# Local and global attention followed by a gated FFN: the gate and value products of the first three FFN blocks are taken during the first half chunk's attention

## The chip, the cores and the metric

The kernel runs on one core of one Trainium2 chip. The metric is the device time of one execution in microseconds (us), as the median of several runs. A core has five engines with queues of their own: TensorE (PE in the profile, with PEld for its weight loads), VectorE (DVE), ScalarE (ACT), GpSimd (POOL) and SyncE (SP), which here issues all DMA transfers. Each queue runs in order.

## What is computed

Eight batches with eight heads each: 512 local queries of width 64 attend to a band of 32 positions to either side and to 32 global keys; 32 global queries attend to all 544 keys. The result, 4,352 rows (8 x 544) of width 512, goes through a gated FFN with 1,536 hidden units.

```python
s_ll = np.where(np.abs(pos[:, None] - pos[None, :]) <= 32, scale * q_l @ k_l.T, -1e9)
a_l = sm(np.concatenate([scale * q_l @ k_g.T, s_ll], axis=-1))
out_l = a_l @ np.concatenate([v_g, v_l])
out_g = sm(scale * q_g @ k_all.T) @ v_all
x = concat([out_g, out_l]).transpose(0, 2, 1, 3).reshape(B * S, H * D)
out = (1 / (1 + np.exp(-(x @ w_gate))) * (x @ w_val)) @ w_out
```

The FFN weights arrive as float64 words and are turned into pairs of float32 parts (high and low) on the chip; a product is the sum of three matmuls: high by high, low by high, high by low.

## The kernel before, in words

**Chunks and blocks.** The local rows are cut into chunks: chunk 0 and chunk 1 are the two halves (256 rows each) of batch 0, chunks 2 to 8 are batches 1 to 7 (512 rows each), and a last chunk of 256 rows holds the global rows. The FFN of a chunk has twelve blocks of 128 hidden units (NF = 12). One FFN item is one chunk and one block f: 12 matmuls into `bank_g` and 12 into `bank_v` (L399: three combinations of parts by four slices kt of the width), the gate on ACT and DVE (L407 to L414: tanh, min, exp, abs), the merge (L419 to L423: two multiplications on DVE, a rounding copy on ACT, a subtraction on DVE, giving `hh`), and one item later the output products (L436) into `bank_o`. Chunk 0 runs eight blocks ahead (`lead`), then chunk 1 its first eight, then both take turns.

**Attention.** A head of chunk 0 is one `local_unit` of four steps: scores (L233), the row minimum on DVE and the exponential on ACT (L247, L250); sums and division (L253, L254, L217) into `p_buf`; transposes on PE (L269) and a copy on ACT (L277); the product with the values (L292, L293) and a copy (L296). After each pair of heads `x_split` (L371 on ACT, L372 on POOL) makes the two parts of slice kt of the FFN's input x: pair kt gives slice kt. In chunk 0 a `fill` of one float32 128x128 matmul stands after three of the four steps, and eight fills stand at the start (L110).

**Converting weights.** `convert` turns one 128x1024-word piece into its two parts: a Prelu on ACT (L136), a shift and a shift-and-or on DVE (L138, L139), a rounding copy on ACT (L140) and a subtraction on POOL (L141). There are 36 pieces (gate, value and output of each block), 512 KB each, in a ring of three staging buffers; when a piece is converted, the load of the piece three places later is issued on SP (`stage`, L126). Output pieces are written back to DRAM (L152, L153) and loaded for use as `wo` (L427).

**The order.** Everything but the FFN items is an event with a due time; `ffn_stream` yields after each group of matmuls how much FFN work it was (4.5 for a half chunk's item), and events that are due by then are emitted in between. Chunk 0's attention is due from -1000 on, four units a head, so that all of it comes before the first FFN item at 0; chunk 1's attention is due from 1 to about 21, chunk 2's from 23 on. The pieces of block 0 are due at -985, -980 and -977, those of block f at -2 + 4f and after. This gives the order of emission; the framework then orders each engine's queue at build time by its own estimate of what is ready, with earlier emitted work first, and `issue_after(ins)` holds an instruction behind `ins` on its engine.

**PSUM.** Eight banks: four for a ring `att`, shared by `bank_x`, `bank_y` (attention), `bank_g` and `bank_v`, and `bank_o0` to `bank_o3`, in which output rows of chunk 0 (o0, o1) and chunk 1 (o2, o3) are summed. Until the first output product these four hold nothing but what the fills write (into o3).

Of the kernel before, what the change touches and what calls it, by code (L numbers as in the profile page):

```python
# [8 lines left out]
F32 = mybir.dt.float32  # L9
# [38 lines left out]
CONVERT = (-2, 4, 1, 3)  # L48
CONVERT_EARLY = (-985, -980, -977)
# [10 lines left out]
def kernel(ctx, tc, qk, v, w_gate, w_val, w_out, out_l, out_g):  # L60
# [45 lines left out]
    fill_ps = ps.tile([P, DM], F32, name="bank_o3")  # L106
# [4 lines left out]

    fill(FILL[0])
# [3 lines left out]
    w_src = []  # L116
    for f in range(NF):
        ws = slice(2 * f * P, 2 * (f + 1) * P)
        w_src += [w.rearrange("(t p) f -> p t f", p=P)[:, :, ws] for w in (w_gate, w_val)]
        w_src.append(w_out[f * P:(f + 1) * P, :].rearrange("(t p) m -> p t m", p=P))  # L120
# [7 lines left out]
    def convert(i, hi, lo):  # L128

        src = w_src[i]  # L130
        t, n = src.shape[1], src.shape[2] // 2
        st, v = (o[i % len(o)].rearrange("p (t n) -> p t n", t=t) for o in conv_bufs)
        words = st.rearrange("p t (n two) -> p t n two", two=2)
        low, high = words[:, :, :, 0], words[:, :, :, 1]
        vf, hf = v.bitcast(F32), high.bitcast(F32)
        nc.scalar.activation(hf, hf, AF.Prelu, scale=2.0 ** -112, alpha=-2.0 ** 32)  # L136
        with tc.issue_after(anchor[0].ins) if i < 3 else nullcontext():
            nc.vector.tensor_scalar(v, low, 29, None, op0=ALU.logical_shift_right)  # L138
            nc.vector.scalar_tensor_tensor(v, high, 3, v, op0=ALU.logical_shift_left, op1=ALU.bitwise_or)  # L139
        nc.scalar.copy(hi, vf)  # L140
        nc.gpsimd.tensor_tensor(lo, vf, hi.bitcast(F32), op=ALU.subtract)  # L141
        stage(i + len(conv_bufs[0]))

    def convert_w(f, i):
        fs = slice(f * P, (f + 1) * P)
        w = (wg, wv)[i]
        convert(3 * f + i, w[0][:, :, fs], w[1][:, :, fs])

    def convert_wo(f):
        hi, lo = (spl.tile([P, 1, DM], F32R, name=nm, tag="kl") for nm in ("wo_hi", "wo_lo"))  # L150
        convert(3 * f + 2, hi, lo)
# [61 lines left out]
    def scaled(kind, out, in_, by):  # L213
        if NORM[kind][cnt["norm"] % len(NORM[kind])] == "s":
            nc.scalar.mul(out, in_, by)
        else:
            nc.vector.tensor_scalar(out, in_, by, None, op0=ALU.mult)  # L217
# [164 lines left out]

    def ffn_stream(items):

        prev = None
        later = []
        wo = None
        for n_it in range(len(items) + 1):
            if n_it < len(items):  # L390
# [3 lines left out]
                for w, nm in ((wg, "bank_g"), (wv, "bank_v")):  # L394
# [9 lines left out]
                    if nm == "bank_g":  # L404
                        th = ffn.tile([P, 512], F32, name="th", bufs=1)[:, 0:ntok]
                        mn = ffn.tile([P, 512], F32, name="mn", bufs=1)[:, 0:ntok]
                        nc.scalar.activation(th, acc, AF.Tanh, scale=0.5)  # L407
                        if n_it < 2 * NF and n_it % 2:
                            nc.scalar.activation(mn, acc, AF.Relu, scale=-1.0)
                            nc.scalar.activation(mn, mn, AF.Exp, scale=-1.0)  # L410
                        else:
                            nc.vector.tensor_scalar(mn, acc, 0.0, None, op0=ALU.min)  # L412
                            nc.scalar.activation(mn, mn, AF.Exp)  # L413
                        last_th = nc.scalar.activation(th, th, AF.Abs)  # L414
                        while later:
                            store_out(*later.pop(0), after=last_th)
                    else:

                        nc.vector.tensor_tensor(acc, acc, mn, op=ALU.mult)  # L419
                        nc.vector.scalar_tensor_tensor(acc, th, 1.0, acc, op0=ALU.add, op1=ALU.mult)  # L420
                        hh = ffn.tile([P, 2, 512], F32R, name="hh", bufs=2)
                        nc.scalar.copy(hh[:, 0, 0:ntok], acc)  # L422
                        nc.vector.tensor_tensor(hh[:, 1, 0:ntok], acc, hh[:, 0, 0:ntok].bitcast(F32), op=ALU.subtract)  # L423
                    yield ntok / 512
                if not (wo is not None and items[n_it - 1][1] == f):
                    wo = ffn.tile([P, 2, DM], F32R, name="wo", bufs=2)
                    nc.sync.dma_start(wo.bitcast(F32), wo_dram[f])  # L427
            if prev is not None:
                C2, f2, ph, pwo = prev
                nt = C2["ntok"] // P  # L430
                if f2 == 0:
                    C2["o"] = [ps.tile([P, DM], F32, name=f"bank_o{C2['o0'] + t}") for t in range(nt)]
                o_ps = C2["o"]
                for i, (a, c) in enumerate(((0, 0), (1, 0), (0, 1))):
                    for t in range(nt):
                        nc.tensor.matmul(o_ps[t], ph[:, a, t * P:(t + 1) * P], pwo[:, c],  # L436
                                         start=f2 == 0 and i == 0, stop=f2 == NF - 1 and i == 2)
                    if f2 == NF - 1 and i == 2:
                        for t in range(nt):
                            if t >= 2 and n_it < len(items):  # L440
                                later.append((C2, t))
                            else:
                                store_out(C2, t)
                    yield nt / 4
            prev = (C, f, hh, wo) if n_it < len(items) else None
# [85 lines left out]
    a0, step, *d = CONVERT  # L531
    for f in range(NF):
        at = a0 + f * step
        g, v_, o = CONVERT_EARLY if f == 0 else (at, at + d[0], at + d[1])
        queue.append((g, 4, lambda f=f: convert_w(f, 0)))
        queue.append((v_, 4, lambda f=f: convert_w(f, 1)))
        queue.append((o, 4, lambda f=f: convert_wo(f)))
# [79 lines left out]
```

## Time and profile before

| | |
|---|---|
| median of 3 runs | 1186.67 us (1185.14 to 1191.4) |
| the profiled execution | 1188.97 us, span of its instructions 1187.1 us |
| first matmul of an FFN item | 38.49 us after the span's start |
| busy, share of the span | PE 97%, PEld 81%, DVE 65%, ACT 64%, POOL 35% |
| granted TensorE clock, mean | 0.997 |

Times within the profile count from the span's start. A row of the timeline is: start, duration from the first start to the last end, engine, line, operation, output and inputs with the shape, count; in brackets the idle time of that engine just before, and what ended it. A float32 matmul of the attention is two passes and counts as two. A row of the windows is: stretch, its length, then busy time and count for PE, PEld, DVE, ACT and POOL, the granted clock, the busy share of the DMA engines and what they moved in GB/s.

### The profile page before, as it was taken

The page shows a single profiled execution, that of the slowest core. Times are in us where ns is not written, and L with a number is a line of the kernel's source. Part 1 is how long each engine was busy: PE and PEld are TensorE (multiplying, and loading weights), DVE is VectorE, ACT ScalarE, POOL GpSimd, SP SyncE. Part 2 cuts the span into 40 slices and gives each one's busy share as a digit, 9 for nine tenths or more (in the row PEclk, how much of TensorE's full clock was granted, in tenths as well). Part 3 has the DMA queues.
Part 4 walks back from the last instruction along what each step waited for, and adds up shares of the span by engine and source line. Part 5 has one row for each costly group of instructions (what it writes and reads, how often), then busy time and mean ns, then how long its engine had stood idle before and what let it go on. Part 6 is the DMA issues. An engine that isn't in the chain of part 4 may idle for free.

```text
span 1187.1 us, 19115 instructions
## 1 busy us (share of the span) xinstructions
PE 1150.8 (97%) x6596; PEld 963.8 (81%) x6596; DVE 776.9 (65%) x2132; ACT 755.0 (64%) x1737; POOL 412.4 (35%) x408
## 2 busy tenths in 40 slices
PE   8898999999999999999999999999999999999998
PEld 6666888888888888887788888888788888888897
DVE  5767756666776676667776677677676677633343
ACT  5897777666666666666666666576665675532333
POOL 1434344424442444434443444434353443100000
PEclk9999999999999999999999999999999999999999
DMA  8787853333333333443333443343443342132143
GB/s 292 251 277 260 260 161 115 115 105 111 115 98 128 115 97 106 115 128 98 109 111 110 115 115 97 106 129 97 115 115 105 112 115 72 49 107 71 54 147 120
DMA packets 59489, 151.81 MB, mean 128 GB/s; under 512 B 6144, under 2 KB 19456, under 8 KB 59392
## 3 DMA queue, kind: packets, MB, share of 16 engines
q1 hardware_dynamic: 59392, 150.59, 41.7%
q8 instruction: 52, 0.85, 0.3%
q14 instruction: 45, 0.37, 0.1%
HBM read 135.36 MB, written 15.20 MB: 127 GB/s over the span
## 4 chain that ended last, share of the span: by engine, by line
PE 70%; DVE 10%; ACT 5%; issue 2%; POOL 1%; DMA 0%; ACTq 0%; DVEq 0%; POOLq 0%
PE bank_v L399 19%; PE bank_g L399 19%; PE bank_o L436 19%; DVE p_buf L217 4%; PE bank_y L269 3%; PE bank_x L233 3%; ACT s_sb L250 3%; PE bank_x L300 2%; PE bank_x L301 2%; PE bank_x L317 1%; PE bank_x L360 1%; DVE t L304 1%; DVE mn L412 1%; DVE bank_v L419 1%; DVE bank_v L420 1%
## 5 line engine op out<-in xcount | busy, mean ns | idle before, releaser
L399 PE MATMUL bank_v<-xt,wv 128*128 128x512 f32 (+1 forms) x1440 | 327.8, 364 | 14.7 <-DVE pt L281 14.4
L399 PE MATMUL bank_g<-xt,wg 128*128 128x512 f32 (+1 forms) x1440 | 331.1, 365 | 1.1 <-DVE hh L423 0.8
L436 PE MATMUL bank_o<-wo,hh 128*128 128x512 f32 x1224 | 330.2, 401 | 0.9 <-ACT hh L422 0.9
L399 PEld LDWEIGHTS bank_v<-xt,wv 128*128 128x128 f32 x1440 | 237.0, 189 | 51.8 <-issue 16.4
L399 PEld LDWEIGHTS bank_g<-xt,wg 128*128 128x128 f32 x1440 | 237.3, 189 | 38.7 <-issue 2.7
L436 PEld LDWEIGHTS bank_o<-wo,hh 128*128 128x128 f32 x1224 | 217.7, 189 | 40.9 <-ACT hh L422 1.8
L250 ACT ACTIVATE s_sb<-s_sb,nm 128x192 f32<-128x192 f32 (+1 forms) x240 | 110.4, 461 | 98.5 <-DVE nm L247 97.6
L217 DVE TENSOR_SCALAR p_buf<-s_sb,r 128x128 f32<-128x128 f32 (+2 forms) x443 | 152.4, 381 | 6.3 <-PE bank_y L269 1.7
L305 POOL TENSOR_TENSOR x<-t 64x256 f32<-64x256 f32 x104 | 76.4, 735 | 173.1 <-DVE t L304 147.0
L210 POOL TENSOR_TENSOR vhl<-v_raw,vhl 128x512 fp32r<-128x512 f32 x52 | 67.2, 1293 | 186.6 <-ACT vhl L209 98.9
L197 POOL TENSOR_TENSOR kl<-qk_raw,qk_hi 128x704 fp32r<-128x704 f32 x52 | 88.6, 1704 | 109.7 <-ACT qk_hi L196 109.2
L422 ACT CAST hh<-bank_v 128x512 fp32r<-128x512 f32 (+1 forms) x120 | 62.7, 523 | 95.4 <-DVE bank_v L420 94.6
L407 ACT ACTIVATE th<-bank_g 128x512 f32<-128x512 f32 (+1 forms) x120 | 63.8, 532 | 85.9 <-PE bank_g L399 85.5
L412 DVE TENSOR_SCALAR mn<-bank_g 128x512 f32<-128x512 f32 (+1 forms) x108 | 67.4, 624 | 72.5 <-ACT th L407 72.5
L304 DVE TENSOR_TENSOR t<-bank_x,t 64x512 f32<-64x512 f32 x104 | 70.7, 680 | 61.9 <-ACT t L303 61.2
L419 DVE TENSOR_TENSOR bank_v<-bank_v,mn 128x512 f32<-128x512 f32 (+1 forms) x120 | 73.6, 613 | 56.6 <-PE bank_v L399 49.8
L247 DVE CUSTOM_DVE_ANT_0 s_sb<-bank_x,masks 128x192 f32<-128x192 f32 (+1 forms) x240 | 79.8, 369 | 37.6 <-PE bank_x L233 32.5
L423 DVE TENSOR_TENSOR hh<-bank_v,hh 128x512 fp32r<-128x512 f32 (+1 forms) x120 | 72.9, 608 | 36.5 <-ACT hh L422 34.6
L199 POOL TENSOR_TENSOR qk_hi<-qk_raw,qk_hi 64x256 fp32r<-64x256 f32 x104 | 80.1, 790 | 4.1
L269 PE MATMUL bank_y<-ident,p_buf 128*128 128x128 f32 x440 | 70.3, 274 | 5.5 <-DVE p_buf L217 3.6
L420 DVE SCALAR_TENSOR_TENSOR bank_v<-th,bank_v 128x512 f32<-128x512 f32 (+1 forms) x120 | 73.2, 610 | 1.8
L413 ACT ACTIVATE mn<-mn 128x512 f32<-128x512 f32 (+1 forms) x108 | 62.9, 582 | 15.8 <-DVE mn L412 11.1
(108 smaller groups left out, 1656.1 us busy)
## 6 DMA issues: line engine op xcount, KB each, us to landing
wo<-wo_dram SPq DMA_DIRECT2D x116, 512.0 KB, 3.4
qk_raw<-in_qk_dram SPq DMA_DIRECT2D x104, 312.0 KB, 4.4
v_raw<-in_v_dram SPq DMA_DIRECT2D x52, 256.0 KB, 2.7
out_dram<-ob SPq DMA_DIRECT2D x34, 256.0 KB, 3.1
xt<-in_w_gate_dram SPq DMA_DIRECT2D x12, 512.0 KB, 5.3
xt<-in_w_val_dram SPq DMA_DIRECT2D x12, 512.0 KB, 5.2
xt<-in_w_out_dram SPq DMA_DIRECT2D x12, 512.0 KB, 4.8
v_nat<-in_v_dram SPq DMA_DIRECT2D x8, 512.0 KB, 7.1
```

Of the source, the lines that this page charges most:

```text
L197: nc.gpsimd.tensor_tensor(kl, t[:, K0:Q1], hi[:, K0:Q1].bitcast(F32), op=ALU.subtract)
L199: nc.gpsimd.tensor_tensor(hi[64:128, r], t[64:128, r], hi[64:128, r].bitcast(F32), op=ALU.subtract)
L217: nc.vector.tensor_scalar(out, in_, by, None, op0=ALU.mult)
L247: anchor[0] = nc.vector.tensor_tensor_reduce(out=s_sb[:, i, w], in0=s_ps[:, i, w], in1=mid[:, w], scale=-0.125, scalar=3.0e38, op0=ALU.add ...
L250: exp_at[0] = nc.scalar.activation(s_sb[:, i, w], s_sb[:, i, w], AF.Exp, bias=nm[:, i:i + 1], scale=-1.0, accum_out=sm[:, i:i + 1])
L269: nc.tensor.transpose(pt_ps[:, t], flat[:, t * P:(t + 1) * P], ident)
L304: nc.vector.tensor_tensor(t0, o_ps[0:64], t0, op=ALU.add)
L399: nc.tensor.matmul(acc, w[a][:, t, fs], xt[:, c, t, x0:x0 + ntok], start=n == 0, stop=n == 11)
L412: nc.vector.tensor_scalar(mn, acc, 0.0, None, op0=ALU.min)
L419: nc.vector.tensor_tensor(acc, acc, mn, op=ALU.mult)
L420: nc.vector.scalar_tensor_tensor(acc, th, 1.0, acc, op0=ALU.add, op1=ALU.mult)
L436: nc.tensor.matmul(o_ps[t], ph[:, a, t * P:(t + 1) * P], pwo[:, c], start=f2 == 0 and i == 0, stop=f2 == NF - 1 and i == 2)
```

## The change

The gate and value products of blocks 0, 1 and 2 for chunk 0 leave the FFN stream. They are taken slice by slice as soon as a pair of heads has given its slice of x (`pre_products`, 6 matmuls for block and slice, 72 in all), and are summed in banks o2, o3 and o1, gate and value side by side in one bank. Since the sums of a bank are then spread over time, each of the three banks is first set to zero by a float32 matmul of `ident` with the zeroed `p_bufs[0]` (128x512). The fills go to o0.

The FFN stream starts with the gates and merges of the three blocks, then takes block 3; the output products of blocks 0 and 1 stand between block 3's gate and value products, that of block 2 after them. Chunk 0's output banks o0 and o1 are opened by block 0's output products, and o1 held block 2's sums. Items 3 to 20 yield 0.5 more each (9 in all, what the 72 matmuls yielded), so that from item 21 on the due times meet the same items as before.

The six gate and value pieces of the three blocks are converted and loaded first, due from -992.9 to -975.5; the output pieces of blocks 0 and 1 follow at -971.5 and -967.5, that of block 2 at -2, block 3 from -3 on and each later block four units after the one ahead. For the first three pieces the Prelu is now held behind the exponential that was emitted last (before it was free), and the DVE steps are held behind the last division step or row minimum (before, the last row minimum). `gate_parts`, `merge`, `load_wo` and `out` hold the code that stood in the stream, with the same instructions.

```diff
-CONVERT = (-2, 4, 1, 3)
-CONVERT_EARLY = (-985, -980, -977)
+CONVERT = (-3, 4, 1, 3)
+PRE = 3
+PRE_AT = (-992.9, -991.5, -987.5, -983.5, -979.5, -975.5)
+PRE_OUT = (-971.5, -967.5, -2)
...
-    fill_ps = ps.tile([P, DM], F32, name="bank_o3")
+    fill_ps = ps.tile([P, DM], F32, name="bank_o0")
...
+    pre_banks = []
+    for i in (2, 3, 1)[:PRE]:
+        bank = ps.tile([P, 2, 256], F32, name=f"bank_o{i}")
+        nc.tensor.matmul(bank, ident, p_bufs[0], start=True, stop=False)
+        pre_banks.append(bank)
     fill(FILL[0])
...
-        nc.scalar.activation(hf, hf, AF.Prelu, scale=2.0 ** -112, alpha=-2.0 ** 32)
+        with tc.issue_after(exp_at[0].ins) if i < 3 else nullcontext():
+            nc.scalar.activation(hf, hf, AF.Prelu, scale=2.0 ** -112, alpha=-2.0 ** 32)
...
-            nc.vector.tensor_scalar(out, in_, by, None, op0=ALU.mult)
+            anchor[0] = nc.vector.tensor_scalar(out, in_, by, None, op0=ALU.mult)
...
+    def pre_products(f, kt):
+        C = chs[0]
+        ntok, x0, xt = C["ntok"], C["x0"], C["xt"]()
+        fs = slice(f * P, (f + 1) * P)
+        bank = pre_banks[f]
+        for i, w in enumerate((wg, wv)):
+            for n, (a, c) in enumerate(((0, 0), (1, 0), (0, 1))):
+                nc.tensor.matmul(bank[:, i], w[a][:, kt, fs], xt[:, c, kt, x0:x0 + ntok],
+                                 start=False, stop=kt == KT - 1 and i == 1 and n == 2)
...
+        for f in range(PRE):
+            half = slice(256 * (f % 2), 256 * (f % 2) + 256)
+            bank = pre_banks[f]
+            hh = hhs[f // 2][:, :, half]
+            gate_parts(bank[:, 0], th[:, half], mn[:, half], f % 2)
+            merge(bank[:, 1], th[:, half], mn[:, half], hh)
+            pend.append((chs[0], f, hh, lambda f=f: wos[f]))
-        for n_it in range(len(items) + 1):
+        for n_it in range(PRE, len(items) + 1):
...
+                        if n_it == PRE:
+                            yield from out(False)
+                            wos[2] = load_wo(2)
+                            yield from out(False)
...
+            if n_it < 7 * PRE:
+                yield 0.5
...
+    for f in range(PRE):
+        for kt in range(KT):
+            at = max(-1000 + START["per0"] * (2 * kt + 1) + STAGES[-1] + 0.5, PRE_AT[2 * f + 1])
+            queue.append((at, 5, lambda f=f, kt=kt: pre_products(f, kt)))
```

More of the change, by code (lines that the diff above doesn't have):

```diff
@@ L383, in ffn_stream, with load_wo, out @@
+    def load_wo(f):
+        t = ffn.tile([P, 2, DM], F32R, name="wo", bufs=2)
+        nc.sync.dma_start(t.bitcast(F32), wo_dram[f])
+        return t
     def ffn_stream(items):
-        prev = None
+        pend = []
         later = []
         wo = None
-        for n_it in range(len(items) + 1):
+        def out(last):
+            C, f, hh, wo = pend.pop(0)
+            nt = C["ntok"] // P
+            if f == 0:
+                C["o"] = [ps.tile([P, DM], F32, name=f"bank_o{C['o0'] + t}") for t in range(nt)]
+            for i, (a, c) in enumerate(((0, 0), (1, 0), (0, 1))):
+                for t in range(nt):
+                    nc.tensor.matmul(C["o"][t], hh[:, a, t * P:(t + 1) * P], (wo() if callable(wo) else wo)[:, c],
+                                     start=f == 0 and i == 0, stop=f == NF - 1 and i == 2)
+                if f == NF - 1 and i == 2:
+                    for t in range(nt):
+                        if t >= 2 and not last:
+                            later.append((C, t))
+                        else:
+                            store_out(C, t)
+                yield nt / 4
+        th = ffn.tile([P, 512], F32, name="th", bufs=1)
+        mn = ffn.tile([P, 512], F32, name="mn", bufs=1)
+        hhs = [ffn.tile([P, 2, 512], F32R, name="hh", bufs=2) for _ in range(2)]
+        wos = {f: load_wo(f) for f in range(2)}
+        for f in range(PRE):
[6 more added lines that the diff above has]
+        for n_it in range(PRE, len(items) + 1):
@@ L424, in ffn_stream @@
                     yield ntok / 512
                 if not (wo is not None and items[n_it - 1][1] == f):
[L426 to L444, printed above, removed]
@@ L445, in ffn_stream @@
-            prev = (C, f, hh, wo) if n_it < len(items) else None
+                    wo = load_wo(f)
+            if pend:
+                yield from out(n_it >= len(items))
+            if n_it < len(items):
+                pend.append((C, f, hh, wo))
+            if n_it < 7 * PRE:
+                yield 0.5
     def att_events(ci, start, per, tail=0):
@@ L530 @@
         queue.append((9 * NF * (ci - 2) + (START["x2"] if ci == 2 else 0), -1, new_x))
[L531 to L537, printed above, removed]
+    for t_, f, kind in order:
+        queue.append((t_, 4, (lambda f=f, k=kind: convert_w(f, k)) if kind < 2 else (lambda f=f: convert_wo(f))))
+    for f in range(PRE):
+        for kt in range(KT):
+            at = max(-1000 + START["per0"] * (2 * kt + 1) + STAGES[-1] + 0.5, PRE_AT[2 * f + 1])
+            queue.append((at, 5, lambda f=f, kt=kt: pre_products(f, kt)))
     queue.append((-1002, 2, lambda: [stage(i) for i in range(3)]))
```

51 lines of the change are left out of this document (32 added, 19 removed).

## Prediction

> **What bounds the kernel now.** I read the page first, then the busy times by stage, then PE's timeline from the start to the second FFN item, then ACT, DVE and POOL beside it. The change touches nothing behind the items of the two half chunks, so these carry the argument.
>
> ```profile
> span 1187.1 us, 19115 instructions
> PE 1150.8 (97%) x6596; PEld 963.8 (81%) x6596; DVE 776.9 (65%) x2132; ACT 755.0 (64%) x1737; POOL 412.4 (35%) x408
> ```
>
> ```profile
> 0.00:38.50 38.50, 31.19 (x193) 24.55 (x193) 25.44 (x96) 23.49 (x63) 10.20 (x19) 1.00 0.81 276
> 38.50:60.00 21.50, 20.70 (x127) 15.85 (x127) 14.00 (x42) 19.45 (x55) 8.85 (x8) 1.00 0.84 265
> ...
> 110.00:115.00 5.00, 3.12 (x18) 1.93 (x17) 4.99 (x12) 3.52 (x13) 2.80 (x2) 0.93 0.88 307
> 115.00:120.00 5.00, 5.00 (x17) 3.25 (x15) 2.60 (x9) 2.53 (x9) 1.27 (x1) 0.50 0.14 23
> 120.00:125.00 5.00, 5.00 (x33) 4.51 (x32) 2.03 (x6) 4.14 (x12) 0.31 (x1) 0.88 0.96 318
> ```
>
> The columns behind the length are PE, PEld, DVE, ACT, POOL, then clock, DMA share and GB/s. The first 38.5 us, chunk 0's attention, I call the prelude. PE is busy 31.19 us of it and idle 7.31. In the stage behind it PE is busy for 20.70 of 21.50 us and ACT for 19.45: both are nearly full, so PE work taken out of that stage shortens it, as long as ACT follows. What matters is whether the prelude has room for that work.
>
> ```profile
> 3.81 1.76 PE L233 MATMUL bank_x<-qk_nat 64*128 64x192 f32 x8 [3.81 <-DMA qk_nat<-in_qk_dram]
> 5.50 4.60 PE L110 MATMUL bank_o<-ident 128*128 128x128 f32 x26
> 11.04 0.49 PE L269 MATMUL bank_y<-ident,p_buf 128*128 128x128 f32 x2 [0.95 <-DVE p_buf L217]
> ...
> 18.12 0.97 PE L233 MATMUL bank_x<-qk_nat 64*128 64x192 f32 x4
> 19.02 0.49 PE L110 MATMUL bank_o<-ident 128*128 128x128 f32 x2
> ...
> 21.54 0.97 PE L233 MATMUL bank_x<-qk_nat 64*128 64x192 f32 x4
> ...
> 32.38 0.74 PE L269 MATMUL bank_y<-ident,p_buf 128*128 128x128 f32 x3 [0.78 <-DVE p_buf L217]
> 32.97 1.06 PE L110 MATMUL bank_o<-ident 128*128 128x128 f32 x8
> 35.12 0.43 PE L292 MATMUL bank_x<-pt_nat,v_nat 128*64 128x128 f32 x2 [1.10 <-ACT pt_nat L277]
> ...
> 37.47 0.43 PE L292 MATMUL bank_x<-pt_first,v_nat 128*64 128x128 f32 x2 [0.68 <-ACT pt_first L277]
> 38.49 0.62 PE L399 MATMUL bank_g<-xt,wg 128*128 128x256 f32 x3
> 39.04 0.97 PE L233 MATMUL bank_x<-qk_nat 64*128 64x224 f32 x4
> 40.14 1.48 PE L399 MATMUL bank_g<-xt,wg 128*128 128x256 f32 x9
> 41.46 1.11 PE L399 MATMUL bank_v<-xt,wv 128*128 128x256 f32 x8
> 42.51 1.05 PE L317 MATMUL bank_x<-qk_nat 64*32 64x256 f32 x4
> ...
> 43.54 0.74 PE L399 MATMUL bank_v<-xt,wv 128*128 128x256 f32 x4
> ```
>
> From one head's scores (18.12) to the next (21.54) a head takes 3.42 us of PE, and no row of the timeline between them shows a wait; three fills of two passes, such as the one at 19.02, are among its work. After the empty start (3.81 us) the bracketed waits are 0.95, 0.78, 1.10 and 0.68 us. So I take PE to be the bound of the prelude too. Work moved there is then carried, not hidden, but for these waits.
>
> **The change, part by part.** *The products in the prelude.* 72 matmuls of 128x256, in twelve groups of six. Where twelve of them run back to back later, one costs 0.12 us:
>
> ```profile
> 228.41 1.44 PE bank_g L399 x12
> ```
>
> So 8.64 us is the least if PE is full. The dearest row is the first triple, 0.55 us from 38.49 to 39.04, 0.18 us each, 13.2 us in all. A group of six is nearer to the run of twelve; its six matmuls are 0.72 us by that row and 1.1 by the triples, and I take 0.82, an estimate near the run with some 0.1 us for the change of shape: **+9.8 us**.
>
> *The zeroing.* Three float32 matmuls of 512 columns and two passes, 3,072 columns, now stand ahead of the eight fills. The 26 early passes (3,328 columns) are thirteen fills, eight of the start and five drawn forward from the heads. Zeroing and eight fills are 5,120 columns: 4.60 us for the first 3,328 as now, and 1,792 at the price of the row of 32.97 (1,024 columns in 1.06 us), 1.85 us, so they end at 11.95 instead of 10.10. Transposes began at 11.04: 0.9 us later, and of the five fills, which come later now (ten passes, 1.3 us), I put half on the path. **+1.5 us**; nothing if the zeroing runs in the empty time before 3.81, 4.2 us if all its columns come at the early price.
>
> *The first Prelu behind the exponentials.* ACT stands still for the first weights before it takes the first exponential, though the first scores were done by 5.57 us (3.81 + 1.76):
>
> ```profile
> 8.69 0.68 ACT L136 ACTIVATE xt<-xt 128x512 f32<-128x512 f32 x1 [6.67 <-DMA xt<-in_w_gate_dram]
> 9.27 0.44 ACT L250 ACTIVATE s_first<-s_first,nm 128x192 f32<-128x192 f32 x1
> ```
>
> Held behind, the Prelu lets the exponentials begin up to 3 us sooner. PE gains only its 0.95 us wait by that, for zeroing and fills are next in its queue until 11.95; that wait is in the sum above. Nothing further: **0**.
>
> *The waits filled.* 0.78, 1.10 and 0.68 us, with products at hand to fill them: **-2.6 us** (bounds 0 and -2.6). Prelude: 9.8 + 1.5 - 2.6 = +8.7; block 3 starts at 47.2 instead of block 0 at 38.49.
>
> *The stage behind.* Block 0's 24 matmuls take 0.55 (to 39.04), 2.37 (40.14 to 42.51) and 0.74 us, 3.66 together. Three blocks: **-11.0 us**; -8.6 at the price of the run of twelve.
>
> *The gates in a bunch.* Three gates and merges now start together, and block 0's output product waits for all three, since bank o1 held block 2.
>
> ```profile
> 42.74 0.36 ACT L407 ACTIVATE th<-bank_g 128x256 f32<-128x256 f32 x1
> ...
> 43.74 0.41 ACT L414 ACTIVATE th<-th 128x256 f32<-128x256 f32 x1
> 44.06 0.40 ACT L413 ACTIVATE mn<-mn 128x256 f32<-128x256 f32 x1
> ```
>
> 0.36 + 0.41 + 0.40, and 0.36 for the merge's copy, of the same size as the tanh: 1.53 us of ACT a block, 4.6 for three. Over it lie block 3's 24 matmuls (2.9 us) and chunk 1's first head (0.97 and 1.05 us): 4.9. With the latency between engines I take **+0.5 us**, 0 to 2; without the cover it would be 4.6.
>
> *The weight pieces.* The same pieces, transfers and stores. SP's order changes only in which piece is behind which, and value and gate pieces of blocks 1 and 2 pass the output pieces of 0 and 1. A wait of a load on the ring holds back what is behind it on SP, attention inputs of chunk 1, which have the whole longer prelude to land. ACT has 15 us free in the prelude (38.50 - 23.49) and can take some pieces earlier; in return later pieces are due one block or more sooner. **0**, with 2 us either way.
>
> Sum: 8.7 - 11.0 + 0.5 = **-1.8 us**. The profiled execution took 1188.97 us, 1.9 around its span and 2.3 above the median of the runs; on the median that is **1184.9 us**, 0.15% less. A measurement of this kernel can tell about 0.5% (5.9 us) from no change, so this is the same.
>
> **Rivals.** *A, the prelude has room.* PE's busy time counts pipelined matmuls from start to end and can hide gaps between small passes. By weight loads PE is busy only 24.55 of 38.50 us, 13.95 free, 10.1 without the empty start, more than the 9.8 of the products. If all of it can be used, the sum is 1.5 - 11.0 + 0.5 = -9.0: 1177.7 us. For it: most passes there are short. Against it: the regular 3.42 us with no wait. The Trainium skill, Perfetto Trace Analysis, section Identifying the Most-Contended Engine, calls matmul busy time a poor measure of headroom and weight-load busy time a better one; by that rule this rival would be the forecast.
>
> *B, the half clock is gone.* From 110 to 125 us the granted clock falls to 0.93, 0.50 and 0.88: 0.35 + 2.5 + 0.6 = 3.45 us lost, right behind a stretch with PE busy 3.12 of 5. All that is shifted now; if no such gap comes up, -1.8 - 3.5 = -5.3: 1181.4 us, about at the edge of what can be told.
>
> *C, slower: PE stands at the products for the low parts from POOL.* A group needs the low part of x and of the weights, and in PE's queue the attention of later heads stands behind it.
>
> ```profile
> 18.77 0.41 ACT L371 CAST xt<-x 128x256 fp32r<-128x256 f32 x1
> 19.26 0.73 POOL L372 TENSOR_TENSOR xt<-x,xt 128x256 fp32r<-128x256 f32 x1 [16.90 <-ACT xt L371]
> 29.78 1.27 POOL L141 TENSOR_TENSOR wo_lo<-xt,wo_hi 128x512 fp32r<-128x512 f32 x1 [1.26 <-ACT pt_first L277]
> 29.84 2.91 DVE L217 TENSOR_SCALAR p_buf<-s_first,r 128x128 f32<-128x128 f32 x4
> ```
>
> After a pair of heads a group can wait 0.41 for ACT, 1.27 for a weight piece ahead on POOL, 0.73 for its own: 2.4 us, 9.6 for four pairs: -1.8 + 9.6 = +7.8, 1194.5 us. It is slower from (5.9 + 1.8) / 4 = 1.9 us a pair on, that is if hardly any work of the next heads stands ahead of the groups. Against it: the build-time order puts ready work ahead, and the first pieces come earlier than now. In its favour, POOL also slows DVE: the four divisions at 29.84 take 2.91 us beside POOL's pieces, and more pieces now fall into the prelude. The Trainium skill, SBUF — State Buffer, section Who interferes with whom, has the shared port of the two as an exclusive lock for a whole instruction; the trace agrees (2.91 us for four), and by it every further piece can cost DVE its 1.27 us.
>
> *D, it doesn't do what it says.* The products, ready or not, are all put behind the last pair. Then the 2.6 us of waits stay: +0.8, 1187.5 us. The due times are spread over the pairs, which speaks against it.
>
> **How the numbers follow.** Forecast 0.36 (its own range 1181.5 to 1189, from the bounds of zeroing, waits and bunch), A 0.32, B 0.08, C 0.17, D 0.07. Faster by over 0.5%: A and half of B, 0.36. Slower: C, 0.17. Within: the rest, 0.47. The range leaves out the far end of A and of C: 1176 to 1193 us.
>
> **What would show it.** Right: block 3's first gate matmul at about 47 us; hardly a bracketed wait of over 0.5 us on PE between 12 and 47; a head step of 3.4 us plus 0.8 for each group in it; ACT's first exponential near 6.5 us; the steady chunks behind unchanged. A: block 3 before 43 us. C: waits of groups on xt, wg or wv from POOL, or a clock under 1.00 before 50 us. The forecast is wrong if the stage behind doesn't give back the 11 us because ACT, already at 90% there, holds block 3 and the following gates.

## The result, and the profile after

The changed kernel takes 1196.93 us (median of five runs, 1194.67 to 1197.88), the kernel before 1186.67 us (1184.95 to 1191.4). The ratio is 1.007 (95% interval 1.0049 to 1.0092): the change makes the kernel slower by 0.7%, where no change (1184.9 us, in a range of 1176 to 1193) was forecast.

The page of the changed kernel, for the lines that opened the prediction:

```profile
span 1192.8 us, 19122 instructions
PE 1157.6 (97%) x6602; PEld 968.5 (81%) x6602; DVE 778.5 (65%) x2132; ACT 755.2 (63%) x1737; POOL 413.8 (35%) x408
```

The span is 5.7 us longer, and PE is busy 6.8 us longer. PE's six instructions more are the zeroing passes. The first matmul of chunk 2's first item, which I call the mark, comes at 244.81 us after the change and at 238.01 before, 6.8 us later; behind it the two kernels do the same work, and the change makes up 1.1 us. The windows up to the mark, of the changed kernel first, with its prelude:

```profile
0.00:47.11 47.11, 41.69 (x252) 31.86 (x253) 33.03 (x105) 29.48 (x73) 16.45 (x24) 1.00 0.82 274
0.00:244.81 244.81, 227.79 (x1513) 185.33 (x1513) 160.62 (x481) 179.41 (x485) 93.18 (x91) 0.97 0.66 210
```

```profile
0.00:238.01 238.01, 220.53 (x1506) 180.76 (x1507) 158.67 (x481) 179.30 (x485) 92.38 (x91) 0.99 0.67 216
```

PE's idle time, length less busy time, is 17.02 us after and 17.48 before. So the change did not make PE wait longer in all; it made PE busy 7.26 us longer, with a lower granted clock (0.97 for 0.99). Some 3.4 us of this are the clock: in the trace of the changed kernel it stands at half four times for 3.4 us, 6.8 us lost, in that of the kernel before once for 6.8 us, 3.4 us lost. The rest is of the size of the zeroing (5.03 us, the row of L117 below). The reader should take from this that a summed idle time says nothing of what the waits do to the clock behind them.

**The start.** PE, DVE and ACT of the changed kernel:

```profile
5.54 5.03 PE L117 MATMUL bank_o<-p_buf,ident 128*128 128x512 f32 x6
10.40 2.39 PE L112 MATMUL bank_o<-ident 128*128 128x128 f32 x20
12.64 0.60 PE L286 MATMUL bank_y<-ident,p_buf 128*128 128x128 f32 x4
...
10.61 0.86 DVE L234 TENSOR_SCALAR p_buf<-s_first,r 128x128 f32<-128x128 f32 x4 [3.04 <-PE bank_o L117]
...
6.16 0.46 ACT L267 ACTIVATE s_first<-s_first,nm 128x192 f32<-128x192 f32 x1 [4.14 <-DVE nm L264]
```

The hold works: the first exponential starts at 6.16 us, before at 9.27. But the zeroing reads `p_bufs[0]`, into which head 0's division writes. The division waits 3.04 us for the zeroing and starts at 10.61 us, where it started at 10.70 before. The first transposes come at 12.64 us, before at 11.04: ten fills (twenty passes) stand between the zeroing and them, where before thirteen fills, and no zeroing, were done by 10.10.

**The end of the prelude.** PE, ACT and DVE around block 3's first gate:

```profile
46.09 0.43 PE L309 MATMUL bank_x<-pt_first,v_nat 128*64 128x128 f32 x2 [1.34 <-ACT pt_first L294]
...
47.11 0.62 PE L476 MATMUL bank_g<-xt,wg 128*128 128x256 f32 x3
...
50.45 0.39 PE L407 MATMUL bank_o<-xt,wg 128*128 128x256 f32 x1 [0.85 <-POOL xt L389]
...
53.02 0.84 PE L407 MATMUL bank_o<-xt,wv 128*128 128x256 f32 x3
...
44.64 0.68 ACT L153 ACTIVATE xt<-xt 128x512 f32<-128x512 f32 x1 [2.78 <-DMA xt<-in_w_val_dram]
...
40.87 2.99 DVE L234 TENSOR_SCALAR p_first<-s_first,r 128x128 f32<-128x128 f32 x4
```

Block 3's gate comes at 47.11 us, where 47.2 was forecast. That the time is met is partly luck: 18 of the 72 products, those of the last slice, come after it, from 49.10 to 53.66. ACT stands 2.78 us at a Prelu for its weights, with the copy that PE waits for (1.34 us) behind it; DVE's four divisions take 2.99 us where the first head's took 0.86. The last triple of products takes 0.84 us where the first one, at 22.33, took 0.62: the clock has fallen to half.

```profile
48.00:50.90 2.90, 2.05 (x11) 1.21 (x10) 1.55 (x6) 1.25 (x4) 2.08 (x3) 1.00 1.04 375
50.90:54.40 3.50, 3.50 (x19) 3.50 (x18) 3.06 (x11) 3.41 (x11) 0.00 (x0) 0.51 0.62 196
```

**The last stretch.** These are windows that hold the same work, up to the mark: of the changed kernel, and then of the kernel before.

```profile
185.40:244.81 59.41, 54.26 (x386) 49.75 (x383) 37.91 (x114) 39.35 (x101) 26.11 (x26) 0.94 0.36 105
```

```profile
184.00:238.01 54.01, 50.66 (x384) 46.60 (x383) 38.48 (x114) 37.67 (x99) 25.91 (x26) 1.00 0.40 120
```

The stretch is 5.4 us longer: 3.6 more of PE's busy time, which is the clock (0.06 of 59.41 us), and 1.8 more idle (5.15 for 3.35). The two waits that do it, in the changed kernel's timeline of PE, and the windows behind them:

```profile
199.93 0.71 PE L476 MATMUL bank_v<-xt,wv 128*128 128x256 f32 x4 [2.41 <-DVE pt L298]
...
227.03 0.35 PE L317 MATMUL bank_x<-pt,vhl 128*128 128x256 f32 x1 [1.87 <-DVE pt L298]
```

```profile
201.20:204.60 3.40, 3.40 (x15) 3.18 (x14) 0.92 (x2) 1.17 (x2) 2.00 (x3) 0.51 0.09 15
228.40:231.80 3.40, 3.40 (x19) 3.40 (x18) 2.32 (x5) 3.00 (x8) 3.11 (x4) 0.50 0.19 74
```

Each wait for the copy of chunk 2's probabilities is followed by 3.4 us at half the clock, 1.7 us lost. In the kernel before the waits of this stretch are four, none longer than 1.4 us, and the clock holds. The view of the waits gives what waited for what, the sum, the count and the longest:

```profile
PE bank_x L300 <- DVE pt L281: 3.4, 4, 1.4
```

**Lateness by equal work.** So that the place of a loss can be seen when the order differs, I added up each kernel's matmul records, each weighted by its columns at full clock (0.83 ns a column for a pass of float32, 0.42 ns for the others, zeroing and fills left out). The table shows how much later than the kernel with the hold alone (run `e2_hold_only`, below) a kernel has done the work that this one has done at the time in the first row. Some records are missing, so steps under 1 us mean little.

| time of the hold alone, us | 20 | 40 | 50 | 60 | 80 | 110 | 140 | 180 | 200 | 230 |
|---|---|---|---|---|---|---|---|---|---|---|
| before | 0.8 | 3.0 | 3.1 | 2.9 | 3.9 | 8.5 | 8.6 | 6.5 | 6.5 | 6.5 |
| the change | 2.9 | 2.3 | 6.5 | 8.0 | 9.8 | 8.5 | 10.7 | 7.9 | 10.6 | 13.3 |
| pieces early, no products (`e6`) | 2.2 | 9.9 | 8.9 | 8.9 | 8.6 | 8.8 | 7.7 | 6.5 | 6.5 | 6.5 |
| one block (`e7`) | 0.8 | 1.0 | 1.1 | 2.7 | 5.1 | 10.6 | 14.9 | 11.9 | 11.9 | 11.9 |
| one block, no zeroing (`e9`) | 1.3 | 0.7 | 2.2 | 3.8 | 6.6 | 11.3 | 16.8 | 14.1 | 14.1 | 14.1 |
| products late (`e10`) | 1.2 | 2.3 | 3.5 | 12.3 | 12.2 | 11.4 | 12.8 | 10.0 | 12.6 | 14.2 |
| yields sooner (`e4`) | 2.5 | 1.9 | 6.4 | 7.9 | 13.1 | 27.2 | 27.0 | 24.0 | 24.0 | 24.0 |
| yields at once (`e11`) | 2.1 | 1.5 | 9.6 | 18.5 | 22.3 | 27.8 | 26.4 | 23.4 | 23.4 | 23.4 |

Against the kernel before, the change is ahead by 0.7 us at 40, behind by 3.4 at 50, 5.1 at 60 and 5.9 at 80, even at 110 (there the kernel before comes to its own drop of the clock, which the change doesn't have), behind by 1.4 at 180 and by 6.8 at the end. So there are two losses, 5.8 us at the end of the prelude (40 to 60) and 5.4 in the last stretch, and one gain of some 4.5, the drop that is gone.

The medians differ by 10.3 us and the profiled spans by 5.7: the profiled execution of the kernel before is 2.3 us above its median, that of the change 2.3 us below. So some 4.6 of the 10.3 us lie in no trace. The profiled run of the kernel before was one with a drop at 114 us (clock 0.997, 1188.97 us). Of its 62 runs beside the experiments, two far slower ones left out, 21 had a clock of 1.000 and took between 1184.6 and 1187.5 us; none of the five runs of the changed kernel had a clock above 0.996. So the gain of some 4.5 us holds against this execution of the kernel before, and not against every one.

### The profile page after: what moved, and what is told of

Read it like the earlier page. It is cut to its first block, busy times and chain, and to the rows that moved or that the text cites. A ratio compares the mean times of both kernels' runs of the same rounds, so it can differ in the third digit from the quotient of the medians.

```text
span 1192.8 us, 19122 instructions
## 1 busy us (share of the span) xinstructions
PE 1157.6 (97%) x6602; PEld 968.5 (81%) x6602; DVE 778.5 (65%) x2132; ACT 755.2 (63%) x1737; POOL 413.8 (35%) x408
## 4 chain that ended last, share of the span: by engine, by line
PE 79%; DVE 11%; ACT 7%; issue 2%; DMA 1%; POOL 0%; ACTq 0%; DVEq 0%
PE bank_v L476 20%; PE bank_g L476 20%; PE bank_o L445 20%; PE bank_x L250 4%; PE bank_y L286 4%; DVE p_buf L234 3%; ACT s_sb L267 2%; PE bank_x L334 2%; PE bank_x L317 2%; PE bank_x L318 2%; PE bank_x L377 1%; DVE xt L156 1%; DVE bank_v L421 1%; DVE bank_v L422 1%; ACT th L411 1%
## 5 line engine op out<-in xcount | busy, mean ns | idle before, releaser
L476 PE MATMUL bank_v<-xt,wv 128*128 128x512 f32 (+1 forms) x1404 | 323.5, 367 | 16.6 <-DVE pt L298 16.6
L476 PE MATMUL bank_g<-xt,wg 128*128 128x512 f32 (+1 forms) x1404 | 327.1, 368 | 0.7 <-DVE pt L298 0.6
L476 PEld LDWEIGHTS bank_v<-xt,wv 128*128 128x128 f32 x1404 | 233.4, 190 | 54.0 <-issue 19.0
L476 PEld LDWEIGHTS bank_g<-xt,wg 128*128 128x128 f32 x1404 | 233.8, 191 | 36.3 <-issue 2.0
L234 DVE TENSOR_SCALAR p_buf<-s_sb,r 128x128 f32<-128x128 f32 (+2 forms) x443 | 155.3, 386 | 6.2 <-PE bank_y L286 1.0
L423 ACT CAST hh<-bank_v 128x512 fp32r<-128x512 f32 (+1 forms) x117 | 61.7, 527 | 105.2 <-DVE bank_v L422 104.3
```

The lines of the kernel that those rows point to most:

```text
L234: anchor[0] = nc.vector.tensor_scalar(out, in_, by, None, op0=ALU.mult)
L476: nc.tensor.matmul(acc, w[a][:, t, fs], xt[:, c, t, x0:x0 + ntok], start=n == 0, stop=n == 11)
```

## The experiments

The ratios are to the kernel before on the same chip, with their 95% intervals.

| run | median us | ratio |
|---|---|---|
| `e1_onepass` | 1199.35 | 1.0102 (1.0076 to 1.0128) |
| `e2_hold_only` | 1180.84 | 0.9941 (0.9919 to 0.9963) |
| `e3_bridge` | 1197.43 | 1.0081 (1.0061 to 1.0102) |
| `e4_pace` | 1204.12 | 1.013 (1.0102 to 1.0157) |
| `e5_hold_block3` | 1201.85 | 1.0097 (1.0067 to 1.0127) |
| `e6_piece_order` | 1188.48 | 0.998 (0.9956 to 1.0004) |
| `e7_one_block` | 1194.73 | 1.0038 (1.0017 to 1.0059) |
| `e8_no_hold` | 1200.97 | 1.0091 (1.0059 to 1.0122) |
| `e9_block0_no_zero` | 1193.65 | 1.0053 (1.0037 to 1.007) |
| `e10_products_late` | 1197.82 | 1.009 (1.0069 to 1.0111) |
| `e11_yield_at_once` | 1204.76 | 1.0155 (1.0134 to 1.0175) |
| `e12_hold_fewer_fills` | 1181.97 | 0.9956 (0.9937 to 0.9975) |
| `e13_hold_lead7` | 1181.55 | 0.9939 (0.9921 to 0.9957) |
| `e14_hold_lead9` | 1179.91 | 0.9929 (0.9913 to 0.9946) |
| `e15_change_lead11` | 1196.0 | 1.0065 (1.005 to 1.008) |
| `e16_no_zero_lead9` | 1193.39 | 1.0045 (1.003 to 1.006) |
| `e17_hold_low_on_dve` | 1183.87 | 0.9952 (0.993 to 0.9974) |
| `e18_change_low_on_dve` | 1193.92 | 1.0035 (1.0025 to 1.0046) |

**Zeroing made cheap.** The three banks are zeroed by matmuls of one pass, from a zero tile of their own, so that no division waits for them.

```diff
+    zr = ffn.tile([P, 512], F32R, name="zr", tag="hh", bufs=2)
+    nc.vector.memset(zr.bitcast(F32), 0.0)
-        nc.tensor.matmul(bank, ident, p_bufs[0], start=True, stop=False)
+        nc.tensor.matmul(bank, zr[:, 0:P], zr, start=True, stop=False)
```

> The changed kernel, but each bank is zeroed by a single-pass matmul (float32r) from a zero tile of its own, instead of a two-pass float32 matmul that reads head 0's division buffer. Theory Z (what the change adds is the zeroing, 4.9 us of TensorE less 1.6 us that the fills save, and 3.4 us of further clock drops; the products themselves are carried at their old price): head 0's division no longer waits for the zeroing (3.0 us), the first transposes move from 12.6 to about 9 us, and the time is 3 to 4 us below the changed kernel, 1.003 to 1.004 of the kernel before. Rival P (pacing: chunk 1's attention ends 11 us later and the FFN stream then waits for it): the prelude ends sooner, the end moves by under 1 us.

1.0102: no gain. At the start the edit does what it should: the first transposes come at 10.46 us instead of 12.64. But block 3's gate comes at 47.65 (47.11 in the change), PE waits 2.24 us up to 45.75 for a copy, and the clock stands at half for 10.2 us from 45.3 and for 6.8 us from 59.0. That the time of the zeroing is the cause falls.

**The hold alone.** The kernel before, with one edit of the change:

```diff
+        with tc.issue_after(exp_at[0].ins) if i < 3 else nullcontext():
             nc.scalar.activation(hf, hf, AF.Prelu, scale=2.0 ** -112, alpha=-2.0 ** 32)
```

> The kernel before, with only the Prelu of the first three pieces held behind the exponential. Theory Z: exponentials start near 6.2 instead of 9.3 us, but the thirteen early fills keep TensorE until 10.1, so the first transposes come at 10.1 to 10.3 instead of 11.0: 0.5 to 1 us gained, 0.999 to 1.000. Rival H (the hold is the useful part, everything in the prelude follows the exponentials): 3 us gained, 0.997.

0.9941. The edit that the prediction put at 0 is worth 0.6% by itself. The windows of its prelude and up to the mark:

```profile
0.00:35.82 35.82, 30.27 (x192) 24.21 (x193) 22.12 (x94) 22.66 (x62) 9.67 (x19) 1.00 0.87 286
0.00:231.49 231.49, 217.63 (x1506) 179.87 (x1507) 155.13 (x481) 178.18 (x485) 93.16 (x91) 0.99 0.70 222
```

The prelude is 2.7 us shorter than before (38.50), PE is idle 5.55 us of it instead of 7.31. Nothing of this is won at the first transposes, which come at 11.14 us, before at 11.04: head 0's division starts 3.1 us sooner (7.61 for 10.70), but PE takes seventeen fills there instead of thirteen.

```profile
5.54 5.76 PE L110 MATMUL bank_o<-ident 128*128 128x128 f32 x34
11.14 0.38 PE L270 MATMUL bank_y<-ident,p_buf 128*128 128x128 f32 x2
```

The gain comes between the later heads: the kernel before is 0.8 us late at 20 us and 3.0 at 40 (table). Up to the mark 6.5 us are gained: idle 13.86 us for 17.48, and busy 2.9 less. The prelude's share of this is shown; that the rest are waits and a drop of the clock which no longer fall together is read from the two traces and is not tried by itself.

**Ten fills more behind the last pair**, to hold the clock up (`queue.append((-962.5, 4, lambda: fill(10)))`).

> The changed kernel with ten more fills emitted ahead of the last slice's products, to keep TensorE busy between 44 and 50 us. Theory Z: the clock drop at 51 us is gone (1.7 us), and the fills lie in about 2 us of waits: 0 to 2 us below the changed kernel. Rival P: no gain, up to 2 us slower by the fills.

1.0081, as the change: no gain. The drop at 51 us is gone, but another stands at 58.3, behind a wait of 3.19 us.

**The 9 units yielded sooner:** `if n_it < 3 * PRE: yield 1.5` in place of `if n_it < 7 * PRE: yield 0.5`.

> The changed kernel, but the 9 units that the stream is to yield more are yielded over items 3 to 8 (1.5 each) instead of items 3 to 20 (0.5 each), so that attention is emitted earlier against the FFN items. Theory Z: within 2 us of the changed kernel, moved by clock drops only. Rival P: 3 us or more below the changed kernel, and chunk 1's last global product clearly before 114 us.

1.013, slower. The trace holds something of use all the same: the stretch up to the mark has the waits of the kernel before, and no drop.

```profile
PE bank_x L317 <- DVE pt L298: 3.3, 4, 1.4
```

**Block 3's Prelus held** behind the copy that ends chunk 0's last head (pieces 8 to 11), so that no Prelu stands ahead of this copy.

> The changed kernel, with the Prelus of the four pieces that follow the prelude's eight also held, behind the copy that ends chunk 0's last head. In the changed kernel ScalarE stands 2.8 us at such a Prelu for its load (to 44.6 us) with the last head's copies behind it, TensorE waits and the clock drops. Theory Q (the prelude with products is set by the weight pieces on ScalarE, VectorE, GpSimd and the load ring, not by TensorE): that wait goes, the last slice's products begin 2 to 3 us sooner, the clock drop at 51 us goes: 3 to 5 us below the changed kernel, 1.003 to 1.005 of the kernel before. Rival V (each block carried costs TensorE time by itself): within 1.5 us of the changed kernel.

1.0097: no gain. The wait of 1.34 us at 46 us is gone, but PE waits 2.98 us for a merge at 61.7, and the clock stands at half from 56.9 to 74.0.

**The order of the pieces alone.** The kernel before with the hold, with the change's order and due times for the pieces of blocks 0 to 2; no product is moved, nothing is zeroed. The edit, of which a part is shown, also holds the DVE steps of the first three pieces behind the last division, as the change does.

```diff
-CONVERT_EARLY = (-985, -980, -977)
+PRE_AT = (-992.9, -991.5, -987.5, -983.5, -979.5, -975.5)
+PRE_OUT = (-971.5, -967.5, -2)
```

> The kernel before with the held Prelu and with the changed kernel's order and due times of the weight pieces of blocks 0 to 2, but no product moved and nothing zeroed; later pieces as before. Theory Q: the early pieces are part of the price; 3 us or more above the hold alone, 0.997 or more. Rival V: the order costs nothing, 0.994 as with the hold alone; the whole price is in the products and the zeroing.

0.998, against 0.9941 for the hold alone: some 4.6 us (0.0039 of 1190; 0.8 to 8.5 by the two intervals). The windows at the end of the prelude:

```profile
25.00:41.00 16.00, 11.42 (x57) 8.54 (x58) 12.53 (x39) 11.37 (x31) 6.30 (x6) 0.74 0.77 261
32.00:50.00 18.00, 15.21 (x59) 12.11 (x60) 9.70 (x31) 11.83 (x30) 5.28 (x6) 0.53 0.59 203
```

Between 25 and 41 us PE is idle 4.6 of 16 us while DVE is busy 12.5, and behind it the clock stands at half for 17 us. Its first gate comes at 42.7 us instead of 35.8. So the pieces that come early (with that hold on DVE) hold up the prelude without any product. Not every run is like the trace: the clocks of the ten runs go from 0.991 to 1.000, and the profiled one had 0.993.

**One block in place of three** (`PRE = 1`; the pieces of the later blocks are due four units sooner than before).

> The changed kernel with one block instead of three taken early (one bank zeroed, 24 products). Rival V: a third of the price of three, linear: between 0.994 (hold alone) and 1.007 at about 0.998 to 0.999. Theory Q: less than a third, since eight pieces need not be in the prelude and ScalarE stands at no load: 0.993 to 0.996, about the hold alone.

1.0038: 11 us more than the hold alone for one block, where three cost 15. The price does not go by the number of products. In its trace the clock stands at half for 6.8 us from 82.8 and again from 137.4 us, 6.8 us lost; with the hold alone there is one drop of 3.4 us, 1.7 us lost.

**The change without the hold.**

> The changed kernel without the hold of the first three Prelus. If the hold's gain (0.6% alone) is contained in the changed kernel, this is about 6 us slower than it, 1.012. If the zeroing hides the hold (head 0's division waits for the zeroing until 10.6 us anyway), it is within 2 us of the changed kernel, 1.005 to 1.009.

1.0091 against 1.007: the hold is worth 2 to 3 us within the change (the intervals overlap), and 7 us by itself. What takes the rest is not shown: the division does wait 3.04 us for the zeroing, but `e1_onepass`, in which it doesn't, is no faster.

**One block without zeroing.** Gate and value of block 0 get a bank each, opened by their first product.

```diff
-    for i in (2, 3, 1)[:PRE]:
-        bank = ps.tile([P, 2, 256], F32, name=f"bank_o{i}")
-        nc.tensor.matmul(bank, ident, p_bufs[0], start=True, stop=False)
-        pre_banks.append(bank)
+    pre_banks = [[ps.tile([P, DM], F32, name=f"bank_o{i}")[:, 0:256] for i in (2, 3)]]
...
-                                 start=False, stop=kt == KT - 1 and i == 1 and n == 2)
+                                 start=kt == 0 and n == 0, stop=kt == KT - 1 and n == 2)
```

> The one-block version, but gate and value of block 0 get an output bank each, so that both are opened by their first matmul and nothing is set to zero. Theory N (the carried products cost what they cost before; what is lost is the zeroing, the pieces that come early and the clock drops that waits bring): without zeroing, and with block 0's two gate and value pieces first as in the kernel before, nothing is left to lose: within 2 us of the hold alone, ratio to before 0.993 to 0.996. Rival S (products between the heads break the rhythm of the attention, whatever else is done): about the one-block version with zeroing, 1.001 to 1.004. Rival Z (zeroing alone): the 3 us of zeroing back but the rest stays, 0.999 to 1.001.

1.0053: theory N falls, and it is not the zeroing. But the lateness by equal work shows that S does not hold either: at 40 us this kernel is 0.7 us late, with products between the heads. They are carried at their price. Nearly all of the loss comes behind the prelude, in single waits and the drops of the clock behind them, such as this one:

```profile
84.32 1.22 PE L441 MATMUL bank_o<-wo,hh 128*128 128x512 f32 x2 [2.31 <-ACT hh L419]
...
82.66 0.62 ACT L153 CAST wv<-xt 128x512 fp32r<-128x512 f32 x1 [1.48 <-DVE xt L152]
83.30 0.57 ACT L334 COPY pg_buf<-bank_x 32x512 f32<-32x512 f32 x1
83.90 0.37 ACT L419 CAST hh<-bank_v 128x256 fp32r<-128x256 f32 x1
...
80.34 1.49 DVE L151 TENSOR_SCALAR xt<-xt 128x512 uint32<-128x512 uint32 x1 [0.59 <-POOL wo_lo L154]
...
80.27 1.28 POOL L154 TENSOR_TENSOR wg<-xt,wg 128x512 fp32r<-128x512 f32 x1
```

PE waits for a merge. DVE was behind with a conversion's shift, which took 1.49 us beside POOL's subtraction (0.41 elsewhere), and ACT had a conversion's copy and one of the attention ahead of the merge's.

```profile
80.00:100.00 20.00, 17.69 (x91) 12.64 (x89) 12.45 (x34) 14.45 (x44) 6.32 (x6) 0.83 0.65 216
```

With the drop of the clock behind the wait, this window loses 3.4 us by the clock alone (0.17 of 20 us).

**All products behind the last pair** (`at = -962.5`).

> The change, but all 72 products are due behind the last pair of heads, so that hardly any stands between the heads; zeroing, order of pieces and everything else stay. Theory N: the same work, and the waits between heads stay empty: 1.007 to 1.010 of before. Rival S (the interleaving is what costs): no product between heads, so most of the loss goes, 0.998 to 1.002.

1.009: no gain. This total does not settle S, for the run has a loss of its own behind the prelude: PE waits 3.74 us at 55.7 for the load of `wo`, and the clock stands at half for 13.7 us (in the table 3.5 us at 50, 12.3 at 60). What speaks against S is the table at 40 us: 2.3, as the change, where the kernel before has 3.0. Rival D of the prediction is priced with this: in all it costs what the change costs, within the intervals.

**The 9 units yielded at once**, ahead of item 3 (`yield 3 * PRE` ahead of the loop).

> The change, but the 9 units that items 3 to 20 yield by halves are yielded at once ahead of item 3, so that the later events meet items 3 to 20 as they do in the kernel before. Theory N: the later events are as good in either place; 1.005 to 1.009 of before. Rival P2 (the shifted events make the waits near 200 and 227 us, each with a clock drop of 1.7 us lost behind it): both gone, 3 to 5 us less, 1.002 to 1.004, with block 3 starting later by the conversions and loads that now stand ahead of it.

1.0155. P2 is right on the two waits and wrong on the time: as in `e4_pace`, the stretch up to the mark has the four short waits and no drop (in the table, lateness no longer grows behind 180 us), but with the events of these units ahead of item 3 it is 12.5 us later than the change already at 80 us (22.3 for 9.8), and the clock stands at half for 30.7 us from 56.3 on.

```profile
PE bank_x L317 <- DVE pt L298: 3.3, 4, 1.3
```

**Three fills at the start in place of eight**, with the hold (`FILL = (3, 1)`).

> The kernel before with the hold on the first three Prelus, and three fills at the start in place of eight. Theory N: with the exponentials 3 us sooner the five fills (1.7 us at the early price) are on the path of PE; without them 0 to 2 us less than with the hold alone, 0.992 to 0.995 of before. Rival (the fills at the start keep the clock from falling): the attention starts at a lower clock and loses more than the fills took, 0.996 to 1.000.

0.9956 against 0.9941: no difference that these runs can tell.

**The length of the lead.** Seven and nine blocks with the hold, eleven with the change, nine with one block and no zeroing (only `lead=8` is edited).

> The kernel before with the hold, and chunk 0 runs seven blocks ahead instead of eight; no product is moved and nothing is zeroed. Theory F (chunk 0's items in the lead are what fills PE while chunk 1's attention and the conversions run, so each block less leaves PE waiting): 4 us or more above the hold alone, 0.997 to 1.003 of before, with new waits and clock drops between 45 and 150 us. Rival G (the number of items in the lead does not matter): as the hold alone, 0.992 to 0.996.

> The kernel before with the hold, and chunk 0 runs nine blocks ahead. Theory F: one block of filler more, so the waits of the hold alone between 40 and 150 us (some 6 us) shrink, 0.990 to 0.994 of before, if the pieces of block 8 come in time. Rival G: as the hold alone, 0.992 to 0.996.

> The change, but chunk 0 runs eleven blocks ahead, so that eight items of the lead are left behind the three that were taken in the prelude, as many as before. Theory F: the filler is back and with it most of the 11 us: 0.996 to 1.001 of before. Rival G: the lead does not matter, and the change stays as it is, 1.005 to 1.010.

> Block 0 alone in the prelude, without zeroing, and chunk 0 nine blocks ahead, so that eight items are left in the lead. Theory F: the 11 us above the hold alone shrink to 0 to 4, 0.993 to 0.998 of before. Rival G: as with eight blocks, 1.003 to 1.007.

0.9939, 0.9929, 1.0065 and 1.0045: each as with eight blocks, within the intervals. F falls in three; the run with the hold and nine blocks (0.9929) fits both F's range and G's. The change with eleven blocks also keeps both waits of the last stretch:

```profile
PE bank_v L476 <- DVE pt L298: 2.4, 1, 2.4
PE bank_x L317 <- DVE pt L298: 1.9, 1, 1.9
```

**The low part of the pieces on DVE** (`nc.vector` for `nc.gpsimd` in the subtraction), with the hold and with the change.

> The kernel before with the hold, and the low part of each weight piece is subtracted on DVE in place of POOL: 36 instructions more on DVE, which beside POOL's 36 (1.27 us each) lost time on its own steps. Theory K (DVE's collisions with POOL make the waits): waits shorter or as many, 0.988 to 0.995 of before. Rival L (DVE is the scarcer of the two and the subtractions, in its queue, hold up minima and divisions): 0.996 to 1.004.

> The change, with the low part of each weight piece subtracted on DVE in place of POOL. Theory K: without the collisions the stage behind the prelude gives back the products, and the change comes within 5 us of the hold alone with the same edit: 0.991 to 0.998 of before. Rival L: the loss against the hold alone stays at 12 us or more, 1.004 to 1.012.

0.9952 and 1.0035. The hold alone loses nothing by it that can be told; for the change the ratio is lower than 1.007, with intervals that just miss each other. The two are now 10 us apart (1193.92 less 1183.87) instead of 15 by their ratios: more than the 5 that K asked for and less than L's 12. So the collisions of DVE and POOL carry at most a part of the loss; this pair does not settle how much.

## Why the prediction was wrong

*PE as the bound of the prelude:* right. Rival A, which took the prelude to have room, would have had block 3 before 43 us; it came at 47.11. The Trainium skill, Perfetto Trace Analysis, section Identifying the Most-Contended Engine, would have made A the forecast; here the matmul busy time was the better guide, since PE's busy time in the prelude rose by 10.5 us (41.69 less 31.19) and the prelude by 8.6.

*Products +9.8:* right as a price. By equal work the change is 0.7 us ahead of the kernel before at 40 us, so the products cost about what they cost before. But only 54 of the 72 were done when block 3 began, so that its gate came at the forecast time is partly luck.

*Zeroing +1.5:* right in size: the first transposes come 1.6 us later (12.64 for 11.04). The prediction looked only at PE's queue and missed that the zeroing reads a buffer into which DVE must write (the division's wait of 3.04 us). What this wait costs in all is open, for `e1_onepass` without it is no faster.

*The held Prelu, 0:* wrong as a price of this edit by itself, which is 7 us, 2.7 of them in the prelude. Its reason, that PE has other work up to the first transposes, held even without the zeroing (11.14 for 11.04); what it left out is the gain behind them. Within the change it is worth 2 to 3 us, with intervals that overlap. As a gain it can't be what made the change slower.

*Waits filled, -2.6, and weight pieces, 0 with 2 either way:* these steps failed. PE's idle time in the prelude fell by 1.9 us (7.31 to 5.42): the three old waits are filled, but new ones came behind the last pairs, 1.34 us for a copy behind a Prelu that waits for its load and 1.1 for POOL, most of it behind block 3's first gate. The early pieces cost some 4.6 us without any product, over twice the bound, though the interval (0.8 to 8.5) takes in the 2. That they cost as much beside the products is not shown.

*The stage behind, -11.0:* right as a price from 60 to 180 us. If the moved products were not given back, lateness by equal work would grow there; against the kernel before it goes from 5.1 to 5.9 at 80, and to 1.4 at 180.

*Where the sum broke:* the step that failed is that the sum priced the moved work and the waits beside it, and put nothing for what the new order does elsewhere. It had no term for two things. The first is the end of the prelude, 5.8 us: the late slice, the waits behind a Prelu and POOL, and the half clock that follows them from 50.9. The drop at 114 us, which rival B would have gained and which is gone, nearly pays for this in these two traces. The second is 5.4 us behind 184 us. The sum followed only the moved work, and chunk 2's attention is due from 23, while items 3 to 20 still yield their halves, so it meets other items than before. The change and its versions with the products late or with eleven blocks ahead, all with half yields up to item 20, have the two waits of 2.4 and 1.9 us; the versions that had yielded all by then don't. That the half yields bring these two waits is shown; that the change would be no slower without them is not, since those versions lost more elsewhere. A version that yields the 9 units evenly over items 3 to 12 was not tried.

*Rivals:* C had the time nearly right (1194.5), but by luck, for its reason bears a small part of it: waits for x's low part from POOL are 1.1 us, not 9.6. B had its place right: the half clock at 114 us is gone; but four drops of 3.4 us come in its stead, near 51, 75, 201 and 228 us. D did not come about, and would have cost little.

*What stays open:* why one block costs 11 us and three cost 15. The waits of the one-block versions lie elsewhere (near 84, 105 and 137 us), and the two longest (2.31 and 2.37 us in `e9`) stand behind steps of a conversion. Zeroing and lead don't explain them. Place of the products, pacing and DVE's collisions with POOL were tried with three blocks only, and do not explain the loss there, the collisions at most a part. One rival was not tried by itself: the pieces of the later blocks are due sooner than before, by four units with one block moved and by thirteen with three (block 3 at -3 instead of 10), beside the same attention of chunk 1.

The best versions are the kernel before with the hold, by itself (0.9941) or with nine blocks in the lead (0.9929); their intervals overlap, and both beat the kernel before and the changed one.

## What to carry to other kernels

Price the edits of a change one at a time, and run the smallest alone: here the hold, put at 0, gained 0.6% when run alone, and the bundle hid it. When due times are moved, follow them to where they meet the old ones again, for a stretch in which no work was moved can still lose as much as the one that was changed (5.4 and 5.8 us here). And reckon, behind a new wait of PE of 2 us, with what the clock may take, here 1.7 us.

## What the runs showed of the hardware

The granted clock falls to half for about 3.4 us or a multiple of it (30.7 us in `e11`), behind a wait that is itself shorter: 2.41 us was enough at 199.93 us and 1.87 at 227.03, while waits of up to 1.4 us in the same stretch of the kernel before brought none. The Trainium skill, TensorE: Matmul & The Clock Gate, section Part 1: The HAM clock gate (the "warmup" mystery), puts the fall behind an idle window of about 3.4 us; the length of the drops agrees with such a window, the length of the waits ahead does not.

Nor does the length of one wait decide. The wait near 227 us, 1.8 to 1.9 us long, stands in the change and in `e1`, `e3`, `e5`, `e8`, `e10` and `e15`; five of the seven traces have a drop behind it, `e8` and `e10` have none. And a wait of 0.90 us, up to 74.54 us, was followed by a drop in the change. In its trace the four drops begin 7, 37 and 8 times 3.41 us apart, as if on a fixed grid; whether the place of a wait on it decides was not tried.

DVE's four divisions took 0.86 us alone and 2.99 beside POOL's subtractions; a shift of a conversion took 1.49 for 0.41. The Trainium skill, SBUF — State Buffer, section Who interferes with whom, has this as an exclusive lock on a shared port, and the trace agrees. Yet with the subtraction on DVE the kernel with the hold took 1183.87 us, the same within the interval: either the collisions lie mostly off the path there, or the 36 instructions more on DVE cost as much; the runs don't tell which.
